# Products of a constant tile ahead of the first scores and in TensorE's planned gaps

## The chip, the cores and the metric

The kernel runs on one core of a Trainium2 chip. The metric is the time of one execution on the device in microseconds (us); of several executions the median is taken. A profile is one execution recorded by the hardware profiler; its span runs from the first to the last instruction and is a little shorter than the time of the same execution.

## The reference

Attention with a threshold, and behind it a two-layer network on the same rows:

```python
scores = scale * np.matmul(q, k.transpose(0, 1, 3, 2))      # (8, 8, 576, 64): batch, head, row, depth
thresh = np.max(scores, axis=-1, keepdims=True) - tau
scores = np.where(scores >= thresh, scores, -1000000000.0)
scores = scores - np.max(scores, axis=-1, keepdims=True)
attn = np.exp(scores)
attn = attn / (np.sum(attn, axis=-1, keepdims=True) + 1e-09)
attn_out = np.matmul(attn, v)
x = attn_out.transpose(0, 2, 1, 3).reshape(4608, 512)
h = x @ w_in                                                # (512, 2048)
g = h * (1.0 / (1.0 + np.exp(-h)))
out = g @ w_out                                             # (2048, 512)
```

## The kernel before

The kernel is a list of operations that a planner puts in order once, before anything runs. Each operation has an engine, a planned duration (`occ`), a priority, the values that it reads and writes, and a function that issues its instructions. `Plan.run` gives every operation a planned start and sorts them by it; `Plan.emit` issues them in that order, so each engine's queue is the planned order and never changes at run time. The waits between engines are set by the framework when the instructions are issued: it follows which tile an instruction writes and reads.

The work goes by visits. A visit is one pair of heads of one batch. Batch 0 is visited twice (visits 0 to 3 take the row tiles 0 and 1 of its four pairs, visits 4 to 7 the row tiles 2, 3 and 4); from visit 8 on, a visit takes all five row tiles of a pair, so visits 8 to 11 are batch 1. For one row tile a visit does the following.

- A score operation on TensorE (PE): products of K and Q into two tiles `s`, one for each head of the pair (L821; 8 products of 288 columns in visits 0 to 3, 12 afterwards). A tile `s` is 2 x 512 floats wide in PSUM, two banks; the scores fill columns 0 to 287 of each bank. There are two buffers of it (`new_s`), so a score operation takes both, and the next has to wait until both have been read.
- The softmax of each of the two tiles: the maximum on VectorE (DVE, L547), a threshold (L550), the exponential on ScalarE (ACT, L555), the mask and sum on DVE (L561), two short operations (L567, L572), the division on ACT (L575). The maximum, the exponential and the mask read `s`. In every queue the tile of head 0 comes ahead of the tile of head 1.
- The result is transposed: in visits 0 to 3 on PE (L600, L601, copied to `wT` on ACT, L604, L610), later by transposing DMAs after a split in two halves of 16 bits (`hl`, ACT or POOL).
- Behind the last row tile, the product with V on PE (L679 in visits 0 to 3, L687 later), written to `x` by ACT (L694) and DVE (L699).

Beside this, in roughly the first 240 us, the 32 chunks of the two weight matrices are read and rebuilt from 64-bit words: POOL scales (L358), DVE joins the bits (L364, L367), PE sums with the constant tile `ones` for the largest value (`wps`, L380), POOL puts the signs in (L391), ACT and DVE split each chunk in two halves of 16 bits (L416, L419). The network follows for each block of rows: h products on PE (L736), tanh and products on ACT and DVE (L743, L746, L751, L754), o products on PE (L773), output.

`ones` is a constant tile of 128 x 128 in bf16, all 1.0, written by DVE at the very start.

Of the kernel before, what the change touches and what calls it, by code (L numbers as in the profile page):

```python
# [11 lines left out]
F32 = mybir.dt.float32  # L12
# [7 lines left out]
P = 128  # L20
# [13 lines left out]
URGENT = -1.0e6  # L34
# [16 lines left out]
class Plan:  # L51
# [11 lines left out]
    def op(self, eng, occ, lat, prio, fn, reads=(), writes=(), part=False, hold=(), after=(), dma=None, name="",  # L63
           lock=False, other=None):

        o = Op()
        o.eng, o.occ, o.lat, o.prio, o.fn, o.dma, o.name = eng, occ, lat, prio, fn, dma, name
        o.lock, o.other = lock, other
        o.idx, o.alloc, deps = len(self.ops), [], set(after)
        for x in reads:  # L70
            deps.update(x.w)
            x.r.append(o)
        for x in writes:
            if not part:
                deps.update(x.w)
                deps.update(x.r)
        deps.discard(o)
        o.vs = list(dict.fromkeys([*reads, *writes, *hold]))
        for x in o.vs:
            if x.pool is not None and x.seq is None:  # L80
                x.seq = self.count[x.pool] = self.count.get(x.pool, -1) + 1
                o.alloc.append(x)
            x.users += 1
        for x in writes:
            if part:
                x.w.append(o)
            else:
                x.w, x.r = [o], []
        o.deps = deps
        self.ops.append(o)  # L90
        return o

    def run(self):
# [89 lines left out]
        self.done = sorted(done, key=lambda o: (o.start, o.idx))  # L183
        return max(o.end for o in done)

    def emit(self):
        for o in self.done:
            for x in o.alloc:
                if x.make is not None:
                    x.t = x.make(x.slot)  # L190
            o.fn()


W_AT = (4.0, 12.0)
W_STEP = 1.0
REPORT = None

VISITS = {
# [7 lines left out]
def attention_moe(  # L206
# [10 lines left out]
    nc = tc.nc  # L217
# [6 lines left out]
    ps_s = ctx.enter_context(tc.tile_pool(name="ps_s", bufs=2, space=PSUM))  # L224
    ps_b = ctx.enter_context(tc.tile_pool(name="ps_b", bufs=1, space=PSUM))

    pl = Plan()
    op = pl.op
# [11 lines left out]
    def tiled(tag, shape, dtype, name, bufs, pool=None):  # L240
        return pl.value(name, tag, lambda slot: (pool or sb).tile(shape, dtype, tag=tag, name=name, bufs=bufs))
# [5 lines left out]
        out=gate, in0=tau_sb, scalar1=0.0, scalar2=0.125, op0=ALU.is_ge, op1=ALU.mult  # L247
# [3 lines left out]
        out=ntau, in0=tau_sb, scalar1=0.0, scalar2=-1.0, op0=ALU.max, op1=ALU.mult  # L251
    )
    ones = const.tile([P, P], BF16, name="ones")
    nc.vector.memset(ones, 1.0)
    ident = const.tile([P, P], F32, name="ident")
    make_identity(nc, ident)

# [71 lines left out]
    def weights(group, prio, step, split_prio, split_step):  # L329
        reads = []  # L330
        for k in range(16):
            i, pr = 16 * group + k, prio + step * k
            weight_chunk(i, pr, reads)
        WSC[group] = scale_ops("io"[group], "_w", wmx[:, 4 * group : 4 * group + 4], reads, prio, False)
        for k in range(16):
            split_chunk(16 * group + k, split_prio + split_step * k, group)
# [105 lines left out]
    def prepare_v(b, at_load, at_max, at_scale, at_split):  # L442
        vmx = const.tile([P, NPAIR], F32, name=f"vmx_{b}")
        maxima = []
        for p in range(NPAIR):
            raw = VRAW[b, p] = tiled("vraw", [P, 2, 5, D], F32, f"vraw_{b}_{p}", 4)
            m = pl.value(f"vm_{b}_{p}")

            def load(raw=raw, p=p):
                nc.sync.dma_start(out=raw.t, in_=vL[b, :, 2 * p : 2 * p + 2])  # L450

            def largest(raw=raw, p=p):
                nc.vector.tensor_reduce(  # L453
                    out=vmx[:, p : p + 1], in_=raw.t, op=ALU.max, axis=AX.XYZ, apply_absolute_value=True
                )

            op("SP", 520, 3600, at_load(p), load, [], [raw], dma=1400, name=f"load_v{b}{p}")
            op("DVE", 735, 820, at_max(p), largest, [raw], [m], name=f"vmax{b}{p}")
            maxima.append(m)

        def extra(sc):
            nc.vector.tensor_scalar(out=xscale, in0=sc[:, 0:1], scalar1=2.0**-12, scalar2=None, op0=ALU.mult)

        VS[b] = scale_ops("v", b, vmx, maxima, at_scale, True, extra if b == 0 else None)
        for p in range(NPAIR):
            raw = VRAW[b, p]
            o = V16[b, p] = tiled("v16", [P, 2, 2, 5, D], F16, f"v16_{b}_{p}", 4)

            def high(raw=raw, o=o):
                nc.scalar.activation(o.t[:, 0], raw.t, AF.Copy, scale=VS[b].t[:, 0:1])  # L470

            def low(raw=raw, o=o):
                nc.vector.scalar_tensor_tensor(  # L473
                    out=o.t[:, 1], in0=raw.t, scalar=VS[b].t[:, 0:1], in1=o.t[:, 0], op0=ALU.mult, op1=ALU.subtract
                )

            op("ACT", 720, 815, at_split(p), high, [raw, VS[b]], [o], name=f"vhi{b}{p}")
            op("DVE", 795, 875, at_split(p), low, [raw, VS[b]], [o], lock=True, name=f"vlo{b}{p}")
# [56 lines left out]

    wT = {}

    def new_s(nm):
        return pl.value(f"s_{nm}", "s", lambda slot: ps_s.tile([P, 2, 512], F32, tag="s", name=f"s_{nm}"))

    def softmax(nm, u, v, parts, s, direct=False):
        w = tiled("w32", [P, S], F32, f"w32_{nm}", 4)
# [254 lines left out]
    visits = [(0, p, kind) for kind in ("low", "high") for p in range(NPAIR)]  # L797
    visits += [(b, p, "all") for b in range(1, B) for p in range(NPAIR)]

    prepare_v(0, lambda p: -80 + p, lambda p: 0.5 + p, 4, lambda p: 14 + p)  # L800
    weights(0, W_AT[0], W_STEP, W_AT[0] + 13, W_STEP)
    weights(1, W_AT[1], W_STEP, W_AT[1] + 16, W_STEP)

    def visit(v, b, p, kind, u):
# [21 lines left out]
        for i in tiles:  # L826
            if i < 4:
                ss = [new_s(f"{v}_{r}{i}") for r in range(2)]

                def score(ss=ss, i=i):  # L830
                    for m in range(len(products)):
                        for j in range(2):
                            for r in range(2):
                                product(ss[r].t, i, m, j, r)

                parts = [[(ha + r, i, 0, P)] for r in range(2)]
            else:
                ss = [new_s(f"{v}_4")]

                def score(ss=ss, i=i):  # L840
                    for m in range(len(products)):
                        for j in range(2):
                            product(ss[0].t, i, m, j, None)

                parts = [[(ha, 4, 0, D), (ha + 1, 4, D, D)]]
            cost = 1050 if direct else 900
            op("PE", cost, cost + 155, u, score, reads, ss, name=f"score{v}_{i}")
            for r, s in enumerate(ss):
                softmax(f"{v}_{r}{i}", u, v, parts[r], s, direct)
                u += 1  # L850
# [13 lines left out]
                moe(b, c0, n)  # L864

    pl.run()
    if REPORT is not None:
        REPORT(pl)
    with tc.manual_schedule():
# [47 lines left out]
```

## Time and profile before

| | |
|---|---|
| time, median of 3 runs (lowest to highest) | 1206.28 us (1203.26 to 1207.05) |
| the profiled execution: time, span | 1205.72 us, 1203.9 us |
| granted TensorE clock, mean of the span | 0.953 |
| busy: PE, DVE, ACT, POOL | 1108.0, 888.9, 806.7, 715.3 us |
| busy share: PE, DVE, ACT, POOL | 92%, 74%, 67%, 59% |

PE is busy nearly all the time from about 240 us on, and with gaps before. The page's slices (40 equal parts of the span, some 30 us each, tenths of the time) show that; a row PEclk beside them has the clock that was granted to TensorE, in tenths of full speed. A line of the timeline has the start in us, the duration in us of all instructions merged in it, the engine, the line of the kernel, the operation, the tiles, and, in brackets, how long the engine sat idle before and what released it.

### The profile page before, as it was taken

The numbers are of one execution on the slowest core, as the hardware profiler recorded it, in microseconds if no ns is written. First come the engines' busy times: TensorE is split into PE (matmuls) and PEld (weight loads), VectorE is DVE, ScalarE is ACT, GpSimd is POOL, SyncE is SP. The second block draws the span as 40 slices with busy tenths as digits, with TensorE's granted clock in tenths as the row PEclk, the third lists the DMA queues.
The fourth block names the chain that finished last, engine by engine and source line by source line (L and its number), as shares of the span: only waits on it lengthen the run. The fifth ranks groups of instructions, "written<-read, shape, count | busy, mean of one in ns | idle before, by whom it ended". The sixth has DMA issues, their size and how long they took to land.

```text
span 1203.9 us, 27207 instructions
## 1 busy us (share of the span) xinstructions
PE 1108.0 (92%) x9816; PEld 863.7 (72%) x9816; DVE 888.9 (74%) x2568; ACT 806.7 (67%) x1473; POOL 715.3 (59%) x930
## 2 busy tenths in 40 slices
PE   4876754799899999999999999999999999999998
PEld 2544543577687777777777777777777787787777
DVE  6798898977797877868695869686877888761331
ACT  5787885667686776767685858676777778561441
POOL 1475776856777666667576666757676787630000
PEclk9886876799999999999999999999999999999999
DMA  8356675566777665665766665666667575630000
GB/s 286 113 157 131 154 173 136 97 129 117 140 129 132 129 124 120 120 116 119 131 117 133 115 136 101 134 113 132 128 107 126 111 141 90 124 66 20 11 11 21
DMA packets 352151, 141.12 MB, mean 117 GB/s; under 512 B 326417, under 2 KB 334609, under 8 KB 352017
## 3 DMA queue, kind: packets, MB, share of 16 engines
q1 hardware_dynamic: 352016, 139.38, 57.2%
q8 instruction: 78, 1.28, 0.5%
q14 instruction: 57, 0.46, 0.1%
HBM read 49.68 MB, written 9.44 MB: 49 GB/s over the span
## 4 chain that ended last, share of the span: by engine, by line
PE 84%; DVE 11%; ACT 2%; issue 2%; DMA 1%; SPq 0%; ACTq 0%
PE o L773 31%; PE h L736 31%; PE s L821 12%; PE a L687 9%; DVE w L561 2%; DVE wst L419 2%; DVE wst L367 1%; DVE sm L547 1%; DVE wst L364 1%; PE a L679 1%; ACT w L555 1%; DVE v L473 1%; DMA vraw<-in_vL 0%; DVE vmx L453 0%; DMA kraw<-in_kT 0%
## 5 line engine op out<-in xcount | busy, mean ns | idle before, releaser
L736 PE MATMUL h<-x,wst 128*128 128x288 f16 (+2 forms) x3072 | 398.2, 289 | 2.0 <-DVE wst L419 2.0
L773 PE MATMUL o<-gbuf,wst 128*128 128x288 f16 (+2 forms) x3072 | 394.9, 287 | 2.0 <-DVE wst L419 2.0
L736 PEld LDWEIGHTS <-wst 128*128 128x128 f16 x3072 | 297.4, 99 | 87.4 <-issue 8.6
L773 PEld LDWEIGHTS <-wst 128*128 128x128 f16 x3072 | 295.4, 98 | 86.6 <-issue 9.6
L629 POOL TENSOR_TENSOR hl<-w,hl 128x512 f16<-128x512 f32 x272 | 319.4, 1174 | 16.0 <-issue 2.4
L623 POOL TENSOR_SCALAR hl<-w 128x576 f16<-128x576 f32 x252 | 170.0, 678 | 236.1 <-ACT w L575 223.1
L575 ACT ACTIVATE w<-w,sm 128x576 f32<-128x576 f32 x288 | 216.5, 770 | 83.2 <-DVE sm L572 53.1
L555 ACT ACTIVATE w<-s,sm 128x576 f32<-128x576 f32 x288 | 207.7, 739 | 81.0 <-DVE sm L547 77.4
L547 DVE TENSOR_REDUCE sm<-s 128x1 f32<-128x576 f32 x288 | 208.4, 748 | 69.9 <-PE s L821 67.9
L561 DVE SCALAR_TENSOR_TENSOR w<-s,sm,w 128x576 f32<-128x576 f32 x288 | 230.4, 812 | 31.5 <-ACT w L555 27.5
L746 DVE SCALAR_TENSOR_TENSOR h<-th,h 128x288 f32<-128x288 f32 (+2 forms) x256 | 117.0, 457 | 71.8 <-ACT th L743 68.5
L743 ACT ACTIVATE th<-h,msc 128x288 f32<-128x288 f32 (+2 forms) x256 | 128.5, 502 | 32.6 <-PE h L736 30.1
L754 DVE SCALAR_TENSOR_TENSOR gbuf<-h,gbuf 128x288 f16<-128x288 f32 (+2 forms) x256 | 115.0, 451 | 32.9 <-ACT gbuf L751 32.7
L751 ACT ACTIVATE gbuf<-h 128x288 f16<-128x288 f32 (+2 forms) x256 | 104.6, 410 | 42.0 <-DVE h L746 41.2
L687 PE MATMUL a<-wT,v 128*64 128x288 f16 (+1 forms) x1680 | 114.4, 295 | 0.1
L821 PE MATMUL s<-khi,qhi 64*128 64x288 f32 (+1 forms) x544 | 91.3, 360 | 24.4 <-DVE w L561 19.5
L687 PEld LDWEIGHTS <-v 128*64 128x64 f16 x1680 | 95.0, 113 | 16.9 <-issue 6.9
L821 PEld LDWEIGHTS s<-khi,qhi 64*128 64x128 f32 (+1 forms) x544 | 51.6, 194 | 68.5 <-issue 64.0
L630 POOL TENSOR_TENSOR hl<-w,hl 128x64 f16<-128x64 f32 x272 | 88.1, 324 | 0.0
L391 POOL TENSOR_TENSOR wst<-wst,wsg 128x512 f32<-128x512 f32 x32 | 41.2, 1295 | 63.0 <-PE wps L380 43.1
L784 ACT ACTIVATE ot<-o,msc 128x288 f32<-128x288 f32 (+2 forms) x64 | 31.9, 498 | 65.8 <-PE o L773 64.5
L699 DVE SCALAR_TENSOR_TENSOR x<-a,x 128x288 f16<-128x288 f32 (+1 forms) x60 | 27.3, 456 | 63.3 <-ACT x L694 63.0
(80 smaller groups left out, 1001.7 us busy)
## 6 DMA issues: line engine op xcount, KB each, us to landing
qraw<-in_qT SPq DMA_DIRECT2D x36, 320.0 KB, 3.2
kraw<-in_kT SPq DMA_DIRECT2D x36, 288.0 KB, 3.0
vraw<-in_vL SPq DMA_DIRECT2D x32, 320.0 KB, 3.2
wraw<-in_w_out SPq DMA_DIRECT2D x16, 512.0 KB, 3.9
out_t<-ot SPq DMA_DIRECT2D x56, 144.0 KB, 2.1
wT<-hl SPq DMA_TRANSPOSE x304, 3.3
gbuf<-in_w_in SPq DMA_DIRECT2D x8, 512.0 KB, 6.0
wraw<-in_w_in SPq DMA_DIRECT2D x8, 512.0 KB, 4.2
```

Of the source, the lines that this page charges most:

```text
L547: nc.vector.tensor_reduce(out=sm.t[:, 0:1], in_=s.t[:, :, :HALF], op=ALU.max, axis=AX.XY, negate=True)
L555: nc.scalar.activation(w.t.rearrange("p (j c) -> p j c", j=2), s.t[:, :, :HALF], AF.Exp, bias=sm.t[:, 0:1])
L561: nc.vector.scalar_tensor_tensor(out=w3, in0=s.t[:, :, :HALF], scalar=sm.t[:, 1:2], in1=w3, op0=ALU.is_ge, op1=ALU.mult, accum_out=sm.t[:, ...
L575: nc.scalar.activation(w.t, w.t, AF.Copy, scale=sm.t[:, 4:5])
L623: nc.gpsimd.tensor_scalar(out=fl[:, 0:S], in0=w.t, scalar1=1.0, scalar2=1.0, op0=ALU.mult, op1=ALU.mult)
L629: nc.gpsimd.tensor_tensor(out=fl[:, 640:1152], in0=w.t[:, 0:512], in1=fl[:, 0:512], op=ALU.subtract)
L687: nc.tensor.matmul(a.t[odd * D : (odd + 1) * D, :n], vt.t[:, lo_v, odd, kv, :], w2[odd].t[:, kw, c0 - base : c0 - base + n], start=(k == 0 ...
L736: nc.tensor.matmul(ph.t[:, :n], wi(c, f, lo_w), X[b].t[lo_x][:, c, c0 : c0 + n], start=(j == 0), stop=(j == 11),)
L743: nc.scalar.activation(th.t[:, :n], ph.t[:, :n], AF.Tanh, scale=scale.t[:, 0:1])
L746: nc.vector.scalar_tensor_tensor(out=ph.t[:, :n], in0=th.t[:, :n], scalar=1.0, in1=ph.t[:, :n], op0=ALU.add, op1=ALU.mult)
L773: nc.tensor.matmul(po.t[:, :n], wo(f, d, lo_w), gs[f].t[:, lo_g, :n], start=(f == 0 and j == 0), stop=(f == NF - 1 and j == 2),)
L821: nc.tensor.matmul(out[:, j, :HALF], q.t[rows, i * P : (i + 1) * P], k.t[rows, j * HALF : (j + 1) * HALF], start=(m == 0), stop=(m == len( ...
```

## The change

One operation `warm` is added at the head of the plan: 60 products of `ones` with itself (the moving operand is one column of it, read 224 times) into columns 288 to 511 of the second bank of a tile `s`. It takes one turn of the two buffers of `s`, with 9 us of planned time on PE. After the planning, `fill` goes through the planned gaps on PE: where a gap begins before 230 us and is longer than 250 ns, it puts as many such products at the start of the gap as take 60% of it, at 95 ns each. They are written into the same columns of whichever tile `s` was taken last. No instruction reads those columns.

```diff
+    def fill(self, eng, until, least, each, make):
+
+        end, out = 0.0, []
+        for o in self.done:
+            if o.eng == eng:
+                n = int(FILL * (o.start - end) / each)
+                if end < until and o.start - end > least and n > 0:
+                    f = Op()
+                    f.eng, f.occ, f.lat, f.name, f.fn, f.alloc, f.vs = eng, n * each, n * each, "fill", make(n), [], []
+                    f.start, f.end, f.idx, f.prio, f.ready = end, end + n * each, o.idx, 0.0, 0.0
+                    out.append(f)
+                end = o.start + o.occ
+        self.done = sorted(self.done + out, key=lambda o: (o.start, o.idx))
+
...
 W_AT = (4.0, 12.0)
 W_STEP = 1.0
+FILL = 0.6
+FILL_UNTIL = 230.0e3
+WARM = 60
...
     ones = const.tile([P, P], BF16, name="ones")
     nc.vector.memset(ones, 1.0)
+    wide = ones[:, 0:1].to_broadcast([P, 224])
...
+    last_s = [None]
+
     def new_s(nm):
-        return pl.value(f"s_{nm}", "s", lambda slot: ps_s.tile([P, 2, 512], F32, tag="s", name=f"s_{nm}"))
+        def make(slot):
+            last_s[0] = ps_s.tile([P, 2, 512], F32, tag="s", name=f"s_{nm}")
+            return last_s[0]
+
+        return pl.value(f"s_{nm}", "s", make)
+
+    def occupied(n):
+
+        def products():
+            for _ in range(n):
+                nc.tensor.matmul(last_s[0][:, 1, 288:512], ones, wide, start=True, stop=True)
+
+        return products
...
+    warm = new_s("warm")
+    op("PE", 9000, 9000, 10 * URGENT, occupied(WARM), [], [warm], name="warm")
+
     prepare_v(0, lambda p: -80 + p, lambda p: 0.5 + p, 4, lambda p: 14 + p)
...
     pl.run()
+    pl.fill("PE", FILL_UNTIL, 250.0, 95.0, occupied)
```

The planned order of all other operations stays as it was, on every engine. In all 693 products are added: 60 at the start and 633 in 59 gaps, the last of which begins at 206 us of planned time. Every product is a weight load of `ones` and a matmul.

Two places on PE follow, each before and after. The names end in running numbers, which the added tile shifts; the first digits behind `s_` are the head (0 or 1) and the row tile. Where an instruction waits, the row says for which engine's counter.

The first place is the first visit: the transpose of the second tile of row tile 0 (`tm_10`, `tl_10`), the sums of a weight chunk (`wps`), and the scores of the next visit. Before:

```order
L600 MATMUL tm_10_256<-ident,w_0_10_200 128x128 [waits Activation_49]
L600 MATMUL tm_10_256<-ident,w_0_10_200 128x128 x3
L601 MATMUL tl_10_257<-ident,w_0_10_200 128x128 [waits PE_49]
L380 LDWEIGHTS ones
L380 MATMUL wps_235<-wst,ones 128x128 [waits DVE_49]
...
L821 MATMUL s_00_286<-kraw_140,qraw_143 128x288 [waits DMAHW7_49,DVE_49]
L821 MATMUL s_10_287<-kraw_140,qraw_143 128x288 [waits DVE_49]
```

With the change (all lines of the file stand further down: L821 is L856, L380 is L398, L600 is L632, the new products are L569):

```order
L632 MATMUL tm_10_369<-ident,w_0_10_304 128x128 x3
L633 MATMUL tl_10_370<-ident,w_0_10_304 128x128 [waits PE_49]
L569 LDWEIGHTS ones
L569 MATMUL s_11_321<-ones 128x224 [waits Activation_49]
...
L398 LDWEIGHTS ones
L398 MATMUL wps_339<-wst,ones 128x128 [waits DVE_49]
...
L856 MATMUL s_00_414<-kraw_201,qraw_204 128x288 [waits DMAHW7_49,DVE_49]
L856 MATMUL s_10_415<-kraw_201,qraw_204 128x288 [waits DVE_49]
```

Seven products stand between the transpose and the sums, and eight more between the sums and the scores. The first of the seven waits for ACT: for the exponential that reads the tile `s_11` into which it writes.

The second place is visit 8, the scores of row tile 2, and behind them those of row tile 3. Before:

```order
L821 MATMUL s_12_1964<-khi_1612,qlo_1827 128x288
L821 MATMUL s_02_1963<-klo_1755,qhi_1654 128x288
L821 MATMUL s_12_1964<-klo_1755,qhi_1654 128x288
...
L821 MATMUL s_03_2012<-khi_1612,qhi_1654 128x288 [waits DVE_49,PE_49]
L821 MATMUL s_13_2013<-khi_1612,qhi_1654 128x288 [waits DVE_49,PE_49]
```

With the change:

```order
L856 MATMUL s_02_2494<-klo_2224,qhi_2119 128x288
L856 MATMUL s_12_2495<-klo_2224,qhi_2119 128x288
L569 LDWEIGHTS ones
L569 MATMUL s_12_2495<-ones 128x224
...
L856 MATMUL s_03_2572<-khi_2041,qhi_2119 128x288 [waits DVE_49,PE_49]
L856 MATMUL s_13_2573<-khi_2041,qhi_2119 128x288 [waits DVE_49,PE_49]
```

Between the two score operations stand 29 products into the tile of head 1. In the built program the framework counts a tile's bank as a whole: the maximum of `s_12` on DVE, which before waited for the last score product, now waits for the last of the 29.

## Prediction

> **What bounds the kernel now.** I read the page's slices first, for where which engine is the bound.
>
> ```profile
> span 1203.9 us, 27207 instructions
> PE   4876754799899999999999999999999999999998
> DVE  6798898977797877868695869686877888761331
> PEclk9886876799999999999999999999999999999999
> ```
>
> PE is full from the ninth slice on. Before that the clock has its low digits, PE has gaps, and DVE stands at 8 to 9. The table by stretches puts numbers to it (columns: the stretch, its length, busy time of PE, weight loads, DVE, ACT, POOL, clock, DMA):
>
> ```profile
> 10.00:240.00 230.00, 151.41 (x1001) 106.57 (x1000) 201.54 (x508) 170.00 (x296) 147.18 (x158) 0.77 0.60 152
> 240.00:300.00 60.00, 60.00 (x544) 45.93 (x543) 45.77 (x127) 42.37 (x79) 37.86 (x50) 1.00 0.63 120
> 300.00:340.00 40.00, 35.99 (x335) 27.34 (x333) 29.76 (x94) 27.06 (x44) 28.56 (x40) 0.91 0.74 138
> 340.00:1204.00 864.00, 860.61 (x7943) 683.75 (x7941) 608.00 (x1834) 566.39 (x1057) 500.99 (x679) 1.00 0.56 105
> ```
>
> Up to 240 us DVE is busy 201.5 of 230 us, PE only 151.4, at a mean clock of 0.77. Behind 240 us PE is full; its one gap there (4 us of 300 to 340) is in a loop that starts on PE itself. So what PE has left at 240 us is fixed, and the end moves by what the stretch before it gains or loses, one for one. In that stretch the queue of DVE decides. The list of waits shows what it lacks (who waits for whom: us in total, times, longest):
>
> ```profile
> DVE sm L547 <- PE s L821: 9.3, 8, 3.6
> DVE x L699 <- ACT x L694: 3.4, 4, 2.3
> DVE w L561 <- ACT w L555: 3.0, 9, 0.5
> DVE v_one L307 <- PE v_ps L304: 2.9, 2, 2.1
> DVE gbuf L754 <- ACT gbuf L751: 2.5, 7, 0.5
> DVE wst L364 <- POOL wst L358: 2.4, 1, 2.4
> DVE h L746 <- ACT th L743: 1.7, 5, 0.5
> ```
>
> These are 25.2 us: no faster PE can give back more than that, and what DVE loses by a new wait, it has no other room to make up.
>
> **The clock.** What half speed costs, by rows of the timeline and of the chain of waits: 8 score products, then 12 h products and 36 o products of 256 columns.
>
> ```profile
> 11.58 2.29 PE L821 MATMUL s<-kraw,qraw 64*128 64x288 f32 x8 [0.45 <-ACT qraw L512]
> 36.23 1.24 PE L821 MATMUL s<-kraw,qraw 64*128 64x288 f32 x8
> 98.81 2.56 PE h L736 x12
> 240.12 4.04 PE o L773 x36
> ```
>
> The same scores take 2.29 us at 11.58 and 1.24 us at 36.23, so the first slice runs at half speed too, although the clock is written as 9 there. 256 columns take 2.56/12 = 0.213 us at half and 4.04/36 = 0.112 us at full speed; 224 columns are 7/8 of it: a new product takes 0.187 or 0.098 us (an estimate from these two rows). Two gaps, and the clock around them:
>
> ```profile
> 72.87 0.42 PE L380 MATMUL wps<-wst,ones 128*128 128x128 bf16 x4 [2.32 <-ACT w L555]
> 87.22 0.58 PE L380 MATMUL wps<-wst,ones 128*128 128x128 bf16 x4 [3.60 <-DVE wst L367]
> 52.60:73.10 20.50, 14.34 (x102) 8.80 (x98) 18.63 (x46) 16.61 (x33) 10.89 (x11) 1.00 0.31 92
> 73.10:80.00 6.90, 6.35 (x34) 4.63 (x32) 6.76 (x17) 5.42 (x11) 5.59 (x5) 0.51 0.56 159
> 80.00:86.80 6.80, 3.62 (x35) 2.39 (x32) 6.16 (x15) 6.60 (x12) 4.98 (x6) 1.00 0.76 242
> 86.80:103.80 17.00, 11.45 (x58) 7.75 (x58) 14.95 (x38) 13.20 (x22) 10.38 (x11) 0.50 0.66 124
> ```
>
> A gap of 2.3 or 3.6 us is followed by 7 or 17 us at half speed. The products fill 60% of each planned gap, so I take the clock to be full over most of the stretch. The Trainium skill, page "TensorE: Matmul & The Clock Gate", section "Why this matters for your kernels", asks for no idle gaps over about 3 us between bursts of matmuls; the trace has the drop after 2.3 us already. By that rule alone the change pays: it is the first rival.
>
> **The gain.** DVE's waits that a PE at full speed shortens, place by place:
>
> ```profile
> 48.56 4.48 PE L679 MATMUL a<-wT,vraw 128*64 128x256 f32 x20 [0.90 <-ACT wT L604]
> 54.24 0.76 DVE L547 TENSOR_REDUCE sm<-s 128x1 f32<-128x576 f32 x1 [3.62 <-PE s L821]
> 103.15 0.76 DVE L547 TENSOR_REDUCE sm<-s 128x1 f32<-128x576 f32 x1 [1.28 <-PE s L821]
> 195.97 0.49 DVE L699 SCALAR_TENSOR_TENSOR x<-a,x 128x320 f16<-128x320 f32 x1 [2.33 <-ACT x L694]
> ```
>
> At 54.24 DVE waited 3.62 us for scores behind 4.48 us of V products, most of them at half speed: 2.0 come back. At 103.15 and in the network's short waits behind it, 2.0. At 195.97, behind 28 V products at half speed, 2.2. The other places by the same reading: 24.7 us 1.5, 44.0 us 0.9, 117.0 us 0.4, 141 to 143 us 0.8, 185.2 us 0.9, 218.6 us 0.8. Sum 11.5 us. Bounds: nothing, if the clock stays low; 16.9 us, if all of the first, second, fifth and last line of the waits go.
>
> **The 60 products at the start.** PE's first instruction in the trace is:
>
> ```profile
> 10.86 0.27 PE L304 MATMUL v_ps<-v_diag,ones 128*128 128x128 bf16 x1 [10.86 <-ACT v_diag L301]
> 13.90 1.42 DVE L547 TENSOR_REDUCE sm<-s 128x1 f32<-128x576 f32 x2
> ```
>
> 60 x 0.187 = 11.2 us at half speed, about 1.4 us too long for the 10.86; with half of them at full speed 8.6 us, hidden in the idle time. The ten behind it cost 0.5 us against the 0.45 us gap and make the first scores 1.05 us shorter. I take 0.5 us gained and count it below.
>
> **The new waits.** This is the larger part. The products go into a bank that the softmax reads, and the built program keeps the order bank by bank: whatever reads the tile of head 1 behind them in the plan waits for the last product, and products behind a reader wait for the reader. Where products follow the scores, the path is now scores, products, maximum of head 1, and DVE stands at that maximum with all its queue behind it. The price is (end of the PE work ahead + products x 0.098 us - start of that maximum in the trace). The first place: scores end at 13.87, 33 products make 17.1; the second maximum of the pair in the last row started at 14.6: 2.5 us. A mask (below), one in the middle and the last one:
>
> ```profile
> 87.82 0.81 DVE L561 SCALAR_TENSOR_TENSOR w<-s,sm,w 128x576 f32<-128x576 f32 x1
> 184.46 0.89 PE L821 MATMUL s<-klo,qhi 64*128 64x288 f32 x4
> 185.17 1.42 DVE L547 TENSOR_REDUCE sm<-s 128x1 f32<-128x576 f32 x2 [1.24 <-PE s L821]
> 217.92 0.89 PE L821 MATMUL s<-klo,qhi 64*128 64x288 f32 x4
> 218.63 1.42 DVE L547 TENSOR_REDUCE sm<-s 128x1 f32<-128x576 f32 x2 [1.30 <-PE s L821]
> ```
>
> 185.35 + 29 x 0.098 = 188.2 against 185.9: 2.3 us. 218.8 + 26 x 0.098 = 221.4 against 219.3: 2.0 us. There are 15 such places (four more where the products end in time): 2.5, 2.3, 2.0, 2.0, 1.8, 1.5, 2.7, 0.9, 0.4, 1.5, 1.3, 1.6, 2.3, 1.6, 2.0, sum 26.4 us. At eight places products between other work hold a mask (L561), for instance three behind the sums at 87.2 (87.80 + 0.3 against 87.82): 0.3 to 0.8 each, 4.9 us. At three, scores stand behind products that wait for a mask: 1.5 us. Gross 32.8 us.
>
> The Trainium skill, page "PSUM — Partial Sum Buffer", section "PSUM bank collisions raise a hardware error", says that a write by TensorE and a read by another engine in one bank collide even at disjoint columns, and wants waits by bank. No run here shows a collision. If columns counted instead, none of these waits would stand, and the sum would be the gain alone, 1194.8 us.
>
> From the 32.8 us comes off what is late for another reason. At full speed the PE work ahead of the products ends earlier: 2.0 of the 2.7 us (28 V products), 0.2 to 0.9 at eight other places, 0.5 at the first; together 7.5. The second place's 2.3 us vanish in DVE's 2.4 us wait for POOL; and 1.2 more in short waits for ACT. That is 11.0 us. And while DVE stands, POOL gets on, for which DVE's weight operations wait inside their own duration:
>
> ```profile
> L364 DVE TENSOR_SCALAR wst<-wst x32: 402/418/1376, 18.7 to 203.8; 128x512 int32<-128x512 int32 x32
> ```
>
> (least, median, longest in ns; L367 and L419 look alike.) With L367 and L419 they take some 20 us over their least durations; a tenth more time for POOL takes about a tenth of it off: 2.0 us. Nothing and 5 us are its bounds.
>
> Of the remaining products most lie in PE's idle time and nobody reads their tile again before they are done: nothing.
>
> **The sum.** 32.8 - 11.0 - 2.0 - 11.5 = 8.3 us slower, 1205.72 + 8.3 = 1214.0 us against the profiled execution. That one is 0.56 us below the median, so the median goes from 1206.28 to 1214.6 us. About 0.3% (3.6 us) is what a measurement here can tell from no change.
>
> **Rivals.**
> - The clock decides, and the waits are half hidden: faster. In most of the 15 places the scores ran at half speed, and there they end 1.05 us earlier (2.29 against 1.24); if DVE reaches the second maximum no earlier than now, 15 x 1.05 us comes off beside the 11.0, and 26.4 becomes about 11. With 16.9 us of gain: 32.8 - 15.8 - 11.0 - 16.9 = -10.9, 1195 us; with 11.5 us of gain 1201 us. It decides where the net of the new waits is under 8 us. For it speaks that the chain of waits runs through PE at the places named; against, that DVE is busy 18.6 of the 20.5 us from 52.6 on, and 201.5 of 230 us overall, but for waits for those very scores, so that it is there when the scores are. Chance 0.24, centre 1199 us.
> - Gain and waits cancel: net waits of 8 to 15 us. 1203 to 1210 us. Chance 0.20.
> - The change doesn't raise the clock (waits of the products for DVE and ACT leave gaps of 2.3 us and more between them). Then each product takes 0.187 us: the 23 places have some 280 products, 25 us more, nothing gained: 32.8 + 25 - 5 = 53, 1259 us; half of that, with the clock partly up, 1233 us. Against it stands that 60% of each planned gap is filled. Chance 0.05.
>
> **How the numbers follow.** My own case has 0.51, centre 1214.6 us and a range of 1210 to 1227 us (gain between 7 and 16, what comes off between 5 and 15). Slower by over 0.3% is 0.51 + 0.05 = 0.56, within 0.20, faster 0.24. The range for 8 in 10 goes from 1198 us, which leaves out the lower half of the first rival, to 1228 us, which leaves out the last one.
>
> **What would show it.** Right: PEclk at 9 in the first eight slices; the waits of DVE at L547 for PE, now 9.3 us, grow to 25 us or more, and a product, not a score, is what the second maximum waits for; DVE still full otherwise; everything behind 240 us the same but later; x (L699) at 196 us no longer late. Wrong: the waits at L547 stay near 10 us, or the first full slice of PE comes earlier than now; or the clock keeps its 5 and 6 digits. The weakest steps are the 11.0 us that come off and the count of waits as additive: DVE late at one maximum may be on time at the next.

## The result, and the profile after

The changed kernel takes 1224.79 us (median of 4 runs, 1224.5 to 1225.87) beside 1206.55 us for the kernel before (4 runs, 1203.26 to 1207.05): ratio 1.0159, 95% interval 1.0140 to 1.0178, 18.2 us slower. The forecast was 1214.6 us in a range of 1198 to 1228: the sign and the range hold, the centre is 10.2 us too low, and the slowdown of 8.3 us that was forecast is less than half of the measured one. The profiled execution took 1224.5 us.

The page's slices, after:

```profile
span 1222.7 us, 28592 instructions
PE   7888786699989999999999999999999999999998
DVE  5888886778689786968696868777786879661431
PEclk8998998999989999999999999999999999999999
```

The clock is up: 8 and 9 in the first eight slices, where it went down to 6 and 7 before. PE is fuller as well. But DVE, which stood at 8 and 9 from the third to the eighth slice, falls to 6 to 8 there, and that is the queue that sets the end. The table by stretches (columns as before: stretch, length, busy time of PE, weight loads, DVE, ACT and POOL, clock, DMA):

```profile
10.00:258.00 248.00, 196.77 (x1634) 156.47 (x1633) 195.48 (x507) 170.05 (x295) 144.08 (x158) 0.91 0.56 141
258.00:1222.00 964.00, 957.25 (x8818) 757.33 (x8815) 684.90 (x2054) 635.63 (x1179) 566.01 (x766) 1.00 0.58 107
```

The work that DVE had done in the 230 us up to 240 us takes until 258 us, at a clock of 0.91 in place of 0.77. From there on PE is full and everything is the same, but 18 us later. DVE's list of waits for 10 to 258 us says what filled the time (who waits for whom: us in total, times, longest):

```profile
DVE sm L579 <- PE s L569: 27.4, 16, 3.9
DVE sm L579 <- PE s L856: 5.2, 7, 1.6
DVE w L593 <- ACT w L587: 3.1, 7, 0.9
...
DVE w L593 <- PE s L569: 2.2, 4, 0.7
DVE h L778 <- ACT th L775: 2.0, 4, 1.0
DVE w L593 <- ACT x L726: 1.2, 1, 1.2
DVE w L593 <- ACT khi L541: 1.1, 1, 1.1
DVE w L593 <- ACT wst L434: 0.8, 1, 0.8
...
DVE w L593 <- ACT qhi L541: 0.6, 1, 0.6
...
DVE w L593 <- ACT wsg L406: 0.2, 1, 0.2
```

The first row is new: the softmax's maximum waits 27.4 us for products, at 16 places. Its wait for scores fell from 9.3 to 5.2 us.

The five rows of the mask (L593) with `x`, `khi`, `wst`, `qhi` and `wsg`, 3.9 us in all, name operations of ACT whose results the mask doesn't read. The list puts a wait down to an engine by the profile's events, and here the name misleads, as the place of `khi` shows:

```profile
43.52 0.67 ACT L541 ACTIVATE khi<-kraw 128x576 fp32r<-128x576 f32 x1
43.67 0.94 PE L569 MATMUL s<-ones 128*128 128x224 bf16 x8 [0.52 <-ACT w L587]
44.70 0.82 DVE L593 SCALAR_TENSOR_TENSOR w<-s,sm,w 128x576 f32<-128x576 f32 x1 [1.10 <-ACT khi L541]
```

ACT had been done at 44.19. The products, into the tile that the mask reads, end at 44.61, and the mask starts 0.09 us later. In all five rows it starts 0.09 to 0.11 us after the last product, as it does in the four that name the product (0.10 or 0.11). No list of a kernel whose products leave the tiles `s` has such a row, nor has that of the kernel before. So they count as waits for products: 6.1 us at masks.

**DVE's queue as a sum.** All of DVE's waits were 25.9 us before (10 to 240) and are 50.3 us after (10 to 258). By kind: products +33.5 (27.4 at maxima, 6.1 at masks), scores -4.1, x -3.1, POOL -2.4, the mask waiting for ACT's exponential +0.1, the network's short ones +0.5. DVE's busy time is 201.5 before and 195.5 after, -6.1, and the few tenths that no list holds -0.4. Sum +18.0 us. That is the difference of the two stretches, which hold the same work (508 and 507 operations of DVE), and it is the difference of the times but for 0.2 us.

Three of the sixteen places, the dearest in the middle, each with the products that the maximum waited for:

```profile
13.03 3.40 PE L569 MATMUL s<-ones 128*128 128x224 bf16 x33
16.46 0.76 DVE L579 TENSOR_REDUCE sm<-s 128x1 f32<-128x576 f32 x1 [2.24 <-PE s L569]
...
189.80 4.47 PE L569 MATMUL s<-ones 128*128 128x224 bf16 x23
194.31 0.76 DVE L579 TENSOR_REDUCE sm<-s 128x1 f32<-128x576 f32 x1 [3.88 <-PE s L569]
...
234.23 2.71 PE L569 MATMUL s<-ones 128*128 128x224 bf16 x26
236.98 0.76 DVE L579 TENSOR_REDUCE sm<-s 128x1 f32<-128x576 f32 x1 [2.00 <-PE s L569]
```

At 236.98 and at 16.46 a product takes 2.71/26 = 0.104 and 3.40/33 = 0.103 us; at 189.80 it takes 4.47/23 = 0.194 us. The clock there:

```profile
187.40:194.20 6.80, 6.14 (x34) 4.68 (x34) 2.59 (x8) 2.74 (x4) 6.80 (x10) 0.50 0.80 213
194.20:197.60 3.40, 1.01 (x10) 0.78 (x11) 3.02 (x11) 1.16 (x2) 2.01 (x3) 1.00 0.52 94
197.60:201.10 3.50, 3.50 (x23) 2.63 (x20) 0.76 (x1) 2.20 (x4) 2.73 (x4) 0.51 0.21 75
```

And what PE did ahead of each of the two halves at 0.50:

```profile
185.80 0.39 PE L398 MATMUL wps<-wst,ones 128*128 128x128 bf16 x4 [2.16 <-DVE wst L385]
...
196.30 0.37 PE L856 MATMUL s<-khi,qhi 64*128 64x288 f32 x1 [2.02 <-DVE w L593]
```

PE stood for 2.16 us for DVE, went on at 185.80, and from 187.40 on it ran at half speed, through the very products that the maximum at 194.31 waited for. DVE was late, so its mask (L593) was late, so PE stood for 2.02 us and ran at half speed once more, through most of the next 29 products (to 201.10 us). The two queues wait for each other in turn.

### The profile page after: what moved, and what is told of

Same layout as the page of the kernel before. It is cut to its first block, busy times and chain, and to the rows that moved or that the text cites. A ratio compares the mean times of both kernels' runs of the same rounds, so it can differ in the third digit from the quotient of the medians.

```text
span 1222.7 us, 28592 instructions
## 1 busy us (share of the span) xinstructions
PE 1162.6 (95%) x10509; PEld 921.2 (75%) x10509; DVE 884.2 (72%) x2568; ACT 806.8 (66%) x1473; POOL 710.8 (58%) x930
## 4 chain that ended last, share of the span: by engine, by line
PE 88%; DVE 6%; ACT 2%; issue 2%; DMA 1%; SPq 0%; ACTq 0%; DVEq 0%
PE o L805 31%; PE h L768 30%; PE s L856 13%; PE a L719 9%; PE s L569 4%; DVE w L593 2%; DVE sm L579 1%; DVE wst L385 1%; ACT w L587 1%; DMA gbuf<-in_w_in 1%; DMA qraw<-in_qT 1%; PE a L711 1%; PE wps L398 1%; DVE wst L382 1%; DVE v L491 0%
## 5 line engine op out<-in xcount | busy, mean ns | idle before, releaser
L768 PE MATMUL h<-x,wst 128*128 128x288 f16 (+2 forms) x3072 | 394.1, 287 | 0.0
L593 DVE SCALAR_TENSOR_TENSOR w<-s,sm,w 128x576 f32<-128x576 f32 x288 | 231.0, 813 | 36.4 <-ACT w L587 26.8
L719 PE MATMUL a<-wT,v 128*64 128x288 f16 (+1 forms) x1680 | 111.6, 291 | 0.0
L856 PE MATMUL s<-khi,qhi 64*128 64x288 f32 (+1 forms) x544 | 87.7, 351 | 20.7 <-DVE w L593 16.3
L569 PEld LDWEIGHTS <-ones 128*128 128x128 bf16 x693 | 72.1, 107 | 23.6 <-issue 17.4
L856 PEld LDWEIGHTS s<-khi,qhi 64*128 64x128 f32 (+1 forms) x544 | 49.6, 188 | 53.3 <-issue 45.1
L569 PE MATMUL s<-ones 128*128 128x224 bf16 x623 | 80.1, 281 | 6.5 <-DVE w L593 3.1
```

The costliest lines, as they stand in the source:

```text
L569: nc.tensor.matmul(last_s[0][:, 1, 288:512], ones, wide, start=True, stop=True)
L593: nc.vector.scalar_tensor_tensor(out=w3, in0=s.t[:, :, :HALF], scalar=sm.t[:, 1:2], in1=w3, op0=ALU.is_ge, op1=ALU.mult, accum_out=sm.t[:, ...
L719: nc.tensor.matmul(a.t[odd * D : (odd + 1) * D, :n], vt.t[:, lo_v, odd, kv, :], w2[odd].t[:, kw, c0 - base : c0 - base + n], start=(k == 0 ...
L768: nc.tensor.matmul(ph.t[:, :n], wi(c, f, lo_w), X[b].t[lo_x][:, c, c0 : c0 + n], start=(j == 0), stop=(j == 11),)
L856: nc.tensor.matmul(out[:, j, :HALF], q.t[rows, i * P : (i + 1) * P], k.t[rows, j * HALF : (j + 1) * HALF], start=(m == 0), stop=(m == len( ...
```

## The experiments

Each kernel was timed in turn with the kernel before. None leaves out any work of the kernel before; they differ in how many products there are, and where and into which bank they go.

**1 and 2. The same products into a bank that nobody reads.** The small results have four banks of their own (the pool `bank`); one of the four is given up for it. A second kernel gives up that bank in the kernel before, without products. In the kernel with products:

```
+    own = ps_b.tile([P, 512], F32, tag="own", name="own")
...
-    pl.pool("bank", 4, False)
+    pl.pool("bank", 3, False)
...
-                nc.tensor.matmul(last_s[0][:, 1, 288:512], ones, wide, start=True, stop=True)
+                nc.tensor.matmul(own[:, 288:512], ones, wide, start=True, stop=True)
```

> The same kind of fill (60 products and 603 in the gaps), but written into a PSUM bank of its own that nobody reads; to free it, the pool of single banks has 3 instead of 4. To be compared with e2, which has the 3 banks and no products. Theory (the loss is DVE waiting for products because they share a bank with the scores): 4 to 11 us below e2, DVE's waits at the maximum for products gone, PEclk at 9 or more. Rival (the products themselves cost, by their time on PE or by what they do to the clock): 8 us or more above e2.

> The kernel before with 3 instead of 4 single banks, no products: the control of e1. Both theories: at or above 1206 us, by 0 to 20 us, since the planner has a bank less.

The second, three banks without products, takes 1215.5 us (ratio to the kernel before 1.0081, 1.0065 to 1.0098). With 663 products into the fourth bank it is 1204.61 us (ratio 0.9993, 0.9982 to 1.0003). The runs of the two do not overlap (1212.7 to 1216.1 and 1201.93 to 1205.83). The stretch of both and DVE's waits of 10 to 245 us, first with products (the maximum is L581 there, the scores L858):

```profile
10.00:240.00 230.00, 197.19 (x1799) 158.70 (x1799) 203.05 (x513) 177.41 (x312) 146.22 (x158) 0.98 0.64 156
DVE sm L581 <- PE s L858: 4.8, 6, 1.3
```

and without:

```profile
10.00:240.00 230.00, 158.86 (x1104) 113.79 (x1105) 196.96 (x493) 171.40 (x301) 139.66 (x151) 0.81 0.58 152
DVE sm L547 <- PE s L821: 7.2, 7, 1.3
```

Products that are read by nobody raise the clock from 0.81 to 0.98 and gain 1215.5 - 1204.6 = 10.9 us, with the 60 at the start among them. No row of the first kernel's list has DVE wait for a product. So the clock's gain is real, and about the size that the prediction gave it (11.5 us), but in another plan: three banks alone are 9.5 us slower than the kernel before, and DVE's waits there are others. So the 10.9 us can't be carried over to the change one for one; in the change's own queue the gain is smaller (below).

**3. Only the bank that PE opens next.** Products go where the next operation of PE opens a small bank anyway, into that bank, from when it is free: 199 products in 16 gaps, and the 60.

```
+                into = [x for x in o.alloc if x.pool == "bank"]
+                end = max([end] + [x.at for x in into])
...
+                to = last_s[0][:, 1, 288:512] if into is None else into.t[:, 0:224]
+                nc.tensor.matmul(to, ones, wide, start=True, stop=True)
```

> 60 products at the start, and 199 products in 16 of the gaps, only where the next PE operation opens a single bank: they are written into that bank, from when it is free, and that operation overwrites them. No softmax reads there. Theory: 1200 to 1206 us, since no maximum or mask waits for a product and part of the half-speed time goes. Rival (products cost as such): a third of the 18 us, 1211 us or more.

1204.06 us, ratio 0.9994 (0.9981 to 1.0007), clock of 10 to 240 us 0.81 (0.77 before). A third of the products without the waits costs nothing, and gains nothing that can be told.

**4. The 60 products at the start alone.**

```
-FILL_UNTIL = 230.0e3
+FILL_UNTIL = 0.0
```

> Only the 60 products at the start, none in the gaps. Theory: 1204 to 1207 us, the first scores take 1.3 us instead of 2.3 and the rest is as before. Rival (the turn that the 60 products take of the score buffers, or their time, holds the start): 1209 us or more.

1203.48 us, ratio 0.9988 (0.9978 to 0.9998), half a microsecond below the expected range: the start isn't what makes the change slow. The first scores, which took 2.29 us before:

```profile
11.94 1.24 PE L856 MATMUL s<-kraw,qraw 64*128 64x288 f32 x8 [0.50 <-ACT qraw L530]
```

They take 1.24 us, as the prediction had it, and start 0.36 us later.

**5. Products only behind the maximum.** A gap is filled only if the maximum of the tile in question has begun by then in the plan.

```
-                if end < until and o.start - end > least and n > 0:
+                if end < until and o.start - end > least and n > 0 and top.get(last, -1.0) < end:
```

> The change without the products that stand ahead of a maximum of their tile in the plan: 60 at the start, some 300 in the gaps, all behind the maximum (exponential and mask may still wait). Theory (the loss is the maximum of head 1 waiting for products): 1200 to 1208 us, the 27 us of waits at the maximum for products gone. Rival (each product costs, wherever it stands): 300/633 of the 18 us, 1214 us.

1208.82 us, ratio 1.0035 (1.0021 to 1.0050). That is 0.8 us above the range of the one theory and 5 us below the other's. Of DVE's waits of 10 to 245 us (maximum L583, scores L860, mask L597):

```profile
DVE sm L583 <- PE s L860: 7.1, 9, 2.0
DVE w L597 <- PE s L573: 5.2, 4, 1.5
```

The maximum waits for no product any more. What is left is the mask, a second reader of the same bank, with 5.2 us, and with 3.3 us more that the list puts down to other operations of ACT, as it did in the change: there too the mask starts 0.10 or 0.11 us after a product. So without the products ahead of a maximum, 4.7 us are left of the change's 18.2, though with fewer products in all and a clock of 0.84 from 10 to 240 us.

**6, 7 and 8. The same places, other numbers of products.** One product in each gap; half as many (0.3 of each gap); and 0.9 of each gap, 1024 products in all.

```
-                n = int(FILL * (o.start - end) / each)
+                n = min(1, int(FILL * (o.start - end) / each))
...
-FILL = 0.6
+FILL = 0.3
...
-FILL = 0.6
+FILL = 0.9
```

> The change with one product instead of 60% of the gap in each of the 59 gaps: the waits between engines stand as in the change, but the products take next to no time. Theory split in two: where products directly follow the scores, nothing is left; where they stand behind other PE work (transposes, sums of weights, V products), the maximum of head 1 still waits for that work, by the trace of before 1.3 to 1.6 us at four places, 1 to 6 us slower than before in all, 1207 to 1212 us. Rival (only the products' length counts): 1204 to 1207 us.

> 30% of each gap instead of 60%. Theory: the waits at the maximum fall from 27 to about 13 us by the same places, part of the clock's gain stays: 1208 to 1216 us. Rival (the loss is from clock swings, which fewer products make worse): 1222 us or more.

> The change with 90% of each gap filled instead of 60%. Theory (each product ahead of a maximum adds its length to DVE's wait, whatever the clock gains): waits at the maximum for products 38 to 46 us instead of 27, 1233 to 1245 us. Rival (27 us is so much because products ran at half speed in gaps that were not filled enough; fuller gaps keep the clock): 1220 to 1229 us.

One each: 1211.16 us (ratio 1.0051, 1.0036 to 1.0067). Half: 1216.03 us (1.0095, 1.0078 to 1.0112), at the upper end of what was expected, with 16.3 us of waits at the maximum where about 13 were. Nine tenths: 1245.95 us (1.0338, 1.0321 to 1.0355), 0.95 us above the expected range, with the waits at the maximum inside theirs. DVE's waits for products in the three:

```profile
DVE sm L579 <- PE s L569: 7.1, 5, 1.8
...
DVE w L593 <- PE s L569: 2.1, 3, 1.4
```

```profile
DVE sm L579 <- PE s L569: 16.3, 14, 2.2
...
DVE w L593 <- PE s L569: 1.8, 4, 0.7
```

```profile
DVE sm L579 <- PE s L569: 39.6, 16, 4.0
DVE w L593 <- PE s L569: 9.6, 7, 2.2
```

With the change between the last two, the maximum's waits are 7.1, 16.3, 27.4 and 39.6 us for 1211.2, 1216.0, 1224.8 and 1246.0 us. The mean clock of the profiled execution, 0.953 before, is 0.945, 0.963, 0.979 and 0.984: among these four, the higher the clock, the slower the kernel. The dearest fill was expected to be told from a theory in which a fuller clock makes up for more products (1220 to 1229 us); it doesn't.

**9. Products into a bank whose sum is still open.** Where a weight sum (`wps`) is being added up in parts, its bank stays open between them and nobody reads it until the last. Products go into its columns 288 to 511, without starting a new sum; the sum reads columns 0 to 127. Elsewhere the rule of experiment 3 holds. All four banks stay, and about 463 products are in gaps.

```
+                if sums is not None:
+                    nc.tensor.matmul(sums.t[:, 288:512], ones, wide, start=False, stop=False)
+                    continue
```

> 60 products at the start and some 460 in the gaps, written where no softmax reads: into columns 288 to 511 of a bank in which a weight sum is still being added up (of which only columns 0 to 127 are read, behind the last sum), else into the bank that the next operation opens. All four banks stay. Theory: the clock's gain that e1 showed against e2 (11 us) without its price: 1195 to 1202 us. Rival (the gain in e1 came from the plan with three banks): 1204 us or more.

```profile
10.00:240.00 230.00, 181.12 (x1532) 144.24 (x1532) 207.11 (x524) 174.51 (x304) 148.32 (x160) 0.90 0.61 152
DVE sm L600 <- PE s L877: 5.3, 6, 1.7
```

1198.93 us, ratio 0.9951 (0.9933 to 0.9969): faster than both kernels. The clock is 0.90, close to the change's 0.91; DVE is busy 207.1 of the 230 us (before 201.5), and no product stands in its list. This and the change differ in where the products go, and in 170 of their number, and lie 25.9 us apart by their medians (some 25 by their ratios, each to its own runs of the kernel before).

**10. The same with 0.9 of each gap** (704 products in gaps).

```
-FILL = 0.6
+FILL = 0.9
```

> The kernel of e8 with 90% of each gap filled instead of 60% (some 700 products in the gaps, none in a bank that a softmax reads). Theory (only the half-speed time left before 240 us, 44 us by the trace of e8, still counts there): a gain of 0 to 4 us on e8, 1194 to 1200 us. Rival (products that stand in PE's way cost more than the clock gives): 1202 us or more.

1201.38 us, ratio 0.9962 (0.9949 to 0.9976). The interval overlaps with that of experiment 9. No gain from more products, and the expected 1194 to 1200 us is missed by 1.4 us.

## Why the prediction was right and wrong

**Right: what bounds, and the mechanism.** DVE's queue up to 240 us sets the end, and its delay goes one for one to the end: 18.0 us in the queue, 18.2 us in the time. The clock rose, though three of the first eight slices read 8 and not 9. A product took the place of a score at the second maximum; the waits there passed 25 us; x at 196 us, late by 2.33 us before, waits for 0.26 us:

```profile
210.21 0.49 DVE L731 SCALAR_TENSOR_TENSOR x<-a,x 128x320 f16<-128x320 f32 x1 [0.26 <-ACT x L726]
```

The first place was sized at 2.5 us, 2.0 after what comes off, and measured 2.24. One sign failed: DVE didn't stay as full as it was (195.5 of 248 us, before 201.5 of 230).

**Right: the gross count, in part by luck.** 26.4 us at 15 maxima and 6.4 us at masks and scores were forecast before anything was taken off; 27.4 us at 16 maxima and 6.1 us at masks were measured. That the maxima agree so well is partly luck: the last five of the list were forecast at 8.8 us and cost 13.0, the ten ahead of them at 17.6, where eleven cost 14.4.

**Wrong: the 11.0 us that come off.** This is the step that failed. The prediction took 11.0 us from the 32.8 us "for what is late for another reason", 7.5 of them since PE's work ahead of the products would end earlier at full speed, and was left with 21.8. Measured are 33.5 us of waits for products less 2.3 us for POOL and ACT, 31.2 us: in the sum, nothing of the 7.5 shows. The rows say this much. At the seventh place of the list, behind 28 V products (3.94 us before), 2.0 of 2.7 us were to come off:

```profile
117.92 2.67 PE L719 MATMUL a<-wT,v 128*64 128x320 f16 x28
...
120.76 1.63 PE L569 MATMUL s<-ones 128*128 128x224 bf16 x15
122.43 0.76 DVE L579 TENSOR_REDUCE sm<-s 128x1 f32<-128x576 f32 x1 [1.97 <-PE s L569]
```

The V products did end earlier, by 1.3 us of their own, but only 0.7 us came off the wait: DVE reached the maximum 2.5 us after they began, and in the kernel before it reached the second maximum 3.4 us after (112.52 to 115.9). At the two dearest places the PE work and the products ran at half speed for all or much of their time (0.194 us a product at 189.80 against the 0.098 taken, 4.33/29 = 0.149 us at 198.23), and the maxima cost 3.88 and 3.68 us, where 1.6 and 2.3 were forecast (the twelfth and thirteenth of the list): 3.7 us more. And at full speed a product takes 0.104 us, 6% above the estimate. So the products' term is 8.2 us too low (33.5 against 32.8 - 7.5 = 25.3). How the rest of it divides by place stays open. The other 3.5 us, for POOL and ACT, came to 2.3: DVE's 2.4 us wait for POOL did vanish, but in its place stands 3.09 us for products (at 26.39), and the mask's waits for ACT's exponential stayed as they were. That is 1.2 us more.

**The gain, in the change itself.** In the change's own queue the gain is only 7.1 us (scores 4.1, x 3.1, the remainder 0.4, less 0.5 in the network) where 11.5 were forecast. As I read the working, it counted the same faster PE twice: as a shorter wait for scores, and as an earlier end of the work ahead of the products at the same places. No run tells the two apart.

**The 2.0 us for POOL.** DVE's busy time fell by 6.1 us, above the 5 us given as a bound. The fall lies where the prediction looked for it: the weight operations L364, L367 and L419 (now L382, L385 and L437) were busy 75.8 us before and 68.9 after, with one operation fewer. That it is time lost in waiting for POOL was not tested apart.

Together: +8.2 (products), +1.2 (POOL and ACT), +4.4 (gain), -4.1 (busy time) = +9.7 us on the 8.3 forecast, 18.0.

**The rivals.** "The clock decides, and the waits are half hidden" held the measured gain, but asked that the net of the new waits be under 8 us, and "Gain and waits cancel" that it be 8 to 15; it is 31.2. "The change doesn't raise the clock" had the clock wrong as a mean (0.91), but right at the dearest place: a product cost 0.194 us there, beside its price of 0.187.

**The rules.** The Trainium skill, page "TensorE: Matmul & The Clock Gate", section "Why this matters for your kernels", asks for no idle gaps over about 3 us. By that rule alone the change would pay, and experiments 1 and 9 show that such products can, where nobody waits for them. The measured gaps differ from the page's figure: 2.16 and 2.02 us already came ahead of half speed, but 2.43 us did not, so the length of the gap alone doesn't decide it:

```profile
219.29 0.39 PE L398 MATMUL wps<-wst,ones 128*128 128x128 bf16 x4 [2.43 <-DVE wst L385]
...
220.58 4.85 PE L569 MATMUL s<-ones 128*128 128x224 bf16 x48
```

The 48 products behind that gap take 4.85/48 = 0.101 us each, full speed. What else decides is shown by no run.

The Trainium skill's page "PSUM — Partial Sum Buffer", section "PSUM bank collisions raise a hardware error", wants waits by bank and not by column; the built programs keep them, and the trace agrees in that 27.4 us of waits at the maximum are for columns that it doesn't read, and are gone wherever the products leave that bank. A collision itself is shown by no run.

## What to carry to other kernels

Work that is only there to keep the clock up is free only if nobody waits for it: before it is placed, list who reads the bank, not the columns, and on which engine that reader stands in the queue. A busy share of 60% in a gap says nothing of that; at 1.7 us each (27.4/16), seven waits on the queue that sets the end eat all of the 10.9 us that the clock gained. A bank whose sum is still open has no reader until its last part; in experiment 9, the fastest kernel here, 350 of the 463 products in gaps stood in such a bank.

## What the runs showed of the hardware that was not expected

- At the two places shown, half speed doesn't lie over the gap ahead of it but over the work behind: from 1.6 us after PE went on, for 6.80 us in which PE was busy for 6.14 (187.40 to 194.20), and 3.50 us in which it was busy throughout (197.60 to 201.10; PE had gone on at 196.30). So a filler placed behind a gap can itself run at half speed.
- The number of products alone doesn't set the clock. With 463 and 704 of them in the gaps (experiments 9 and 10) it is 0.90 and 0.92 from 10 to 240 us, and the larger number gained nothing; with 603 in the gaps of the plan with three banks (experiment 1), it is 0.98. The row of experiment 10:

```profile
10.00:240.00 230.00, 194.89 (x1747) 161.24 (x1746) 204.68 (x519) 173.28 (x301) 145.71 (x158) 0.92 0.61 152
```

- A sum in columns 0 to 127 of a bank goes on while products without a start of their own go to columns 288 to 511 of it. In experiment 9, 17 of them take 1.83 us, 0.108 each; 17 of the change's products into a tile `s` also take 1.83 us (at 215.03 us):

```profile
193.55 1.83 PE L588 MATMUL wps<-ones 128*128 128x224 bf16 x17
```
